# Weight halves all on VectorE, a count in PSUM, and a later routing set-up

## The chip, the cores and the metric

The kernel runs on one core of a Trainium2 chip. A core has TensorE (PE), which multiplies matrices into PSUM, VectorE (DVE), ScalarE (ACT), GpSimd (POOL) and SyncE (SP); they run side by side, each through its own list of instructions in order, and wait for one another by semaphores. Here SP issues the loads and most stores, and POOL the indirect gathers and scatters. The metric is the device time of one execution in microseconds (us).

## The reference

Three layers follow one another, all in float32 (B = 2, S = 768, width D = 384):

```python
# 1 gated linear attention, 8 heads of 48
for t in range(S):
    state = alpha[:, :, t, :, None] * state + einsum('bhd,bhe->bhde', k[:, :, t], v[:, :, t])
    y[:, :, t] = einsum('bhd,bhde->bhe', q[:, :, t], state)
# 2 mixer: a token layer (d_tok 256), a channel layer (d_ch 1536)
u = x + (relu(x^T @ w_tok1) @ w_tok2)^T
z = u + relu(u @ w_ch1) @ w_ch2
# 3 experts: 8 of 384 -> 1024 -> 384, one for each token
logits = z @ w_gate;  local = sigmoid(z @ w_local)
e = argmax(logits) if local < 0.5 or s == 0 else e of the token before
out = softmax(logits)[e] * (relu(z @ w1[e]) @ w2[e])
```

## The kernel before

**Products in parts.** Where float32 precision is wanted, `parts` (L337) makes one product of three: high half by high half, high by low, low by high. Every weight is split on its way: ACT casts the raw tile to the high half (L333), and an engine that the call of `split` names subtracts it from the raw tile, which gives the low half (L334, a TENSOR_TENSOR with both inputs in SBUF). Activations are split likewise: ACT writes `hh`, DVE `hl` (L509 and L510 in the mixer, L820 and L821 in the experts); there one of the inputs lies in PSUM.

**Attention** runs over 16 half-steps (2 batches, 4 pairs of heads, 2 halves of the sequence). Per half SP loads a block with decays, keys and queries (L180), and `v` (L184) once for both halves. DVE makes two scans (L191, L197), POOL scales keys and queries (L217, L218), PE makes scores, states and outputs, with products of ones between them in the first half-steps (L164). The tables for the routing are made in `route_setup`, the gate's weights loaded in `route_load` (L569). A few products of the mixer's first layer (`mix_hiddens`) are issued in the last half-steps.

**Mixer.** The token layer for both batches, then the channel layer over groups of 384 tokens (`h` and `a` products of L337). While it runs, the tokens of earlier groups are routed, and the first expert's weights arrive (`expert_weights`): of each expert three tiles of `w1` and four of `w2`, each tile in two halves. DVE takes the low halves of `w1` and of the even halves of `w2`, POOL those of the odd ones.

**Closing** is the end of the mixer: the last 384 tokens leave the channel layer (sums `a` by PE, `u` of L489 by DVE, `x2d` stored by SP), and are routed one group of 128 after the other, in a chain of small operations through PE, DVE and ACT (L612 to L717). Beside it `close` starts expert 0 on the tokens it already has; `fill_half` (L889) counts how many places are left over there, on one element (L893 to L899). Around it three tiles of expert 1's weights are split, with `w1_eng` set to POOL for the low halves.

**Experts** 1 to 7 have two tiles of 128 tokens each. PE makes a hidden product `h` per 128 of the 1024 hidden units, and adds its second product into `o` one or two steps later; DVE's `y` (L807) is scattered to the output by POOL (L729). Gathers (L725) fetch the tokens. `more_passes` and L1253 look whether a further pass is needed, again on one element.

**Order.** The program is written per stage with priorities and `issue_after` bounds; a scheduler turns it into one list per engine. Tile names are those of the buffers, so that weights of different experts appear as c0h, c1h, x0h, x1h, th (high) and c0l, c1l, x0l, x1l, tl (low).

Of the kernel before, what the change touches and what calls it, by code (L numbers as in the profile page):

```python
# [10 lines left out]
ALU = mybir.AluOpType  # L11
AX = mybir.AxisListType

P = 128
# [5 lines left out]
NG = 2  # L20
# [13 lines left out]
KD = DM // P  # L34
# [57 lines left out]
class Build:  # L92
# [79 lines left out]
    def attention_load(self, h):  # L172

        nc, n = self.nc, h["n"]
        x = self.ring[n % len(self.ring)][:DQ]
        src = self.i["akq"][h["b"], h["p"], h["g"]]
        cuts = [0, NA + 1, NA + 1 + SG, NA + 1 + 2 * SG]

        for lo, hi in zip(cuts, cuts[1:]) if n == 0 else [(0, cuts[3])]:
            nc.sync.dma_start(x[:, lo:hi], src[:, lo:hi])  # L180
        h["alpha"], h["k"], h["q"] = [x[:, lo:hi] for lo, hi in zip(cuts, cuts[1:])]
        if h["g"] == 0:
            h["v"] = self.vs[n // NG % len(self.vs)]
            nc.sync.dma_start(h["v"], self.i["v"][h["b"], h["p"]].rearrange("t c (j d) -> t c j d", j=2))  # L184

    def att_decay(self, h):

# [96 lines left out]
    def attention(self, x, between):  # L284
        hs = []
        for b in range(B):
            for p in range(NP):
                for g in range(NG):
                    hs.append({"b": b, "p": p, "g": g, "x": x, "n": len(hs)})
        n = len(hs)  # L290
        state = None

        def load(h):
            self.attention_load(h)
            if h["g"]:
                h["v"] = hs[h["n"] - 1]["v"]

        def decay(h):

            after = hs[0].get("scaled" if h["n"] == 1 else "scored") if h["n"] in (1, 2) else None  # L300
            with self.tc.issue_after(after.ins) if after is not None else nullcontext():
                self.att_decay(h)

        def add(h):
            nonlocal state

            with self.tc.issue_after(hs[min(h["n"] + 2, n - 1)]["back"].ins):
                state = self.att_state(h, state if h["g"] else None)

        stages = {"L": load, "D": decay, "I": self.att_back, "Q": self.att_scale,  # L310
                  "K": self.att_knat, "C": self.att_scores, "S": add, "O": self.att_out}
        done = set()

        def go(x, k):
            if 0 <= k < n and (x, k) not in done:
                done.add((x, k))
                with self.tc.high_priority(offset=PRI[x]) if x in PRI else nullcontext():
                    stages[x](hs[k])

        for x in "LDIQ":  # L320
            go(x, 0)
        for i in range(-5, n):
            for x in ORDER.split():
                go(x[0], i + int(x[1:]))
            if i >= 0:
                between(i, hs)
# [409 lines left out]
    def expert_weights(self, experts, to):  # L736


        nc = self.nc

        def load(j):
            e, i = experts[j // STEPS_W], j % STEPS_W
            pool, tag, bufs = self.stages[j % len(self.stages)]
            if i < KD:
                x = self.t(pool, [P, FF], tag, bufs=bufs)
                src = self.i["moe2_w1"][bass.ds(e, 1)]
                nc.sync.dma_start(x, src[:, i * P:(i + 1) * P].rearrange("o p f -> p (o f)"))
            else:
                f = 2 * (i - KD)
                x = self.t(pool, [P, 2, DM], tag, bufs=bufs)  # L750
                src = self.i["moe2_w2"][bass.ds(e, 1)]
                nc.sync.dma_start(x, src[:, f * P:(f + 2) * P].rearrange("o (k p) d -> p (o k) d", p=P))
            return x

        got = []
        for n in range(len(experts)):
            n1, n2 = self.ROOM[n % len(self.ROOM)]
            size = KF // len(n2)
            for i in range(STEPS_W):
                while len(got) < len(self.stages) and n * STEPS_W + i + len(got) < len(experts) * STEPS_W:  # L760
                    got.append(load(n * STEPS_W + i + len(got)))
                x = got.pop(0)
                if i == 0:
                    w1 = [self.big_tile(n1 + y, [P, KD, FF], F32R) for y in "hl"]
                    w2, rest = [], []
                    to[n] += [w1, w2, rest]
                if i < KD:
                    for m in range(0, FF, PART):
                        ms = slice(m, m + PART)
                        self.split(w1[0][:, i, ms], w1[1][:, i, ms], x[:, ms], self.w1_eng)  # L770
                else:
                    for f in range(2):
                        if len(w2) == 2 * (i - KD) + f:
                            room = size if len(n2) == 1 else NT
                            h, l = [self.big_tile(n2[len(w2) // size] + y, [P, room, DM], F32R) for y in "hl"]
                            w2 += [(h[:, k], l[:, k]) for k in range(size)]
                            if room > size:
                                rest += [y[:, size:].rearrange("p n d -> p (n d)") for y in (h, l)]
                        self.split(*w2[2 * (i - KD) + f], x[:, f], nc.gpsimd if f else nc.vector)
                yield  # L780

    def expert_input(self, xs, to):
# [106 lines left out]
    def fill_half(self):  # L889

        nc, t, rp = self.nc, self.t, self.rtp
        ps = self.room(1)
        nc.tensor.matmul(ps[0:1], self.onesb[:, 0:1], self.count[:, 0:1], start=True, stop=True)  # L893
        more = t(rp, [P, 1], "fill")
        nc.vector.tensor_scalar(more[0:1], ps[0:1], -1.0, float(P), ALU.mult, ALU.add)
        nc.vector.tensor_scalar(more[0:1], more[0:1], 0.0, None, ALU.max)
        x = t(rp, [P, E], "sum", BF16, bufs=CG)
        nc.vector.tensor_copy(x, self.count)
        nc.vector.tensor_tensor(x[0:1, 0:1], x[0:1, 0:1], more[0:1], ALU.add)  # L899
        self.count = x  # L900
# [157 lines left out]
    def mixer_and_experts(self, x, r0, weights):  # L1058


        nc = self.nc
        self.stages = [(self.stp, "part", 2), (self.stp, "raw64", 2)] * 2
        self.ahead = AHEAD
        self.w1_eng = nc.vector
        with self.phase():
            self.mixp = self.pool("mix", 2)
            self.psh = self.pool("ps_h", 2, space=PSUM)
# [51 lines left out]
            def aside(n, m):  # L1119
                if n == 0:  # L1120
                    more()
                if n + 1 < B * NG and 3 <= m < 3 + CG:
                    if m == 3:
                        turns[n] = self.turn(us[n + 1], uts[n + 1])
                    next(turns[n])
                if n and m:
                    if m == 1:
                        routes[n] = self.route((n - 1) * CG, [us[n - 1][:, c] for c in range(CG)], self.room)
                    next(routes[n], None)
                if n and m % 3 == 0:  # L1130
                    if next(later, None) is not None:
                        next(stream)
                if n == B * NG - 1 and m == CLOSE:
                    early.append(self.close(ws[0]))
                    next(early[0])
                if n == B * NG - 1 and m == MC - 1:

                    self.w1_eng = nc.gpsimd
                    for _ in range(AHEAD_W):
                        next(stream)  # L1140
                    self.w1_eng = nc.vector

            chains, weighs, early = [], [], []

# [147 lines left out]
def mixed(ctx, tc, ins, out):  # L1292
# [16 lines left out]
    with z.phase():  # L1309
        z.attention_setup()  # L1310
        z.bits = lambda: z.t(z.psp["bits"], [P, PART], "bits")
        z.warm_up(WARM)
        steps = B * NP * NG

        def between(i, hs):
            if i == 1:
                z.route_setup()
                z.route_load()
            if i == 0:
                next(weights)  # L1320
            if i % 2 and i // 2 < EARLY:
                with tc.high_priority(offset=-BEHIND), tc.issue_after(hs[min(i + 3, steps - 1)]["back"].ins):
                    next(weights)
            if i == NP * NG - 1:
                x.append(inputs(1))
            if i == steps - 5:
                z.load_to = 12
            if i == steps - 3:

                r = z.hidden_room()  # L1330
                ahead.extend((r, z.mix_hiddens(x[0], lambda: z.t(z.psp["r"], [P, 512], "r")[:, :DM], r)))
            if i >= steps - 3:
                for _ in range(KT * NT // 3):
                    next(ahead[1])

        z.attention(x, between)
        for _ in ahead[1]:
            pass
        z.bad_decay()
# [49 lines left out]
```

## Time and profile before

| what | value |
|---|---|
| time, median of 3 runs | 459.81 us (457.43 to 463.89) |
| profiled execution, its own time | 459.7 us |
| its span, first to last instruction | 458.0 us |
| PE busy | 428.0 us (93%) |
| DVE, ACT, POOL busy | 284.1, 178.9, 149.0 us |
| DMA | 56.11 MB, 123 GB/s on average |

The span leaves out what lies before the first and after the last instruction, here 1.7 us. Busy times overlap: they don't add up to the span. A row of a timeline gives start and length, and in brackets how long the engine had been idle and what released it; an instruction that takes several times as long as others of its shape, with no idle time before it, was held up while it ran.

### The profile page before, as it was taken

How to read it: one execution, taken by the hardware profiler on the slowest of the kernel's cores; microseconds unless marked ns; L12 is line 12 of the kernel's file. 1: busy time of each engine (PE TensorE's matmuls, PEld its weight loads, DVE VectorE, ACT ScalarE, POOL GpSimd, SP SyncE). 2: the span in 40 equal slices, each digit the busy share in tenths (PEclk: the TensorE clock that was granted, in tenths of full speed). 3: DMA queues.
4: the chain of work that ended last, by engine and by line, in shares of the span. 5: the costliest groups of instructions: out<-in, count | busy, mean ns of one | idle time of the engine just before them, and what ended most of it. 6: DMA issues, size and time to landing. Idle time of an engine off the chain costs nothing. (4 is left out here: it accounts for less than half of the span.)

```text
span 458.0 us, 7912 instructions
## 1 busy us (share of the span) xinstructions
PE 428.0 (93%) x2938; PEld 387.6 (85%) x2938; DVE 284.1 (62%) x672; ACT 178.9 (39%) x439; POOL 149.0 (33%) x169
## 2 busy tenths in 40 slices
PE   6999999999999999999999985999898998998991
PEld 3577788779999999999999975678888998998990
DVE  5999993499994335134431475666977968928320
ACT  3646664323355231122112140256655555625210
POOL 3767772443442000000000033077527325405010
PEclk9899999999999999999999997999999999999996
DMA  8999976141348300010001004059777847410010
GB/s 213 259 250 247 240 281 230 48 136 47 93 135 252 115 1 0 1 52 1 0 8 47 1 10 133 34 181 281 207 242 247 254 135 247 134 37 28 3 45 24
DMA packets 27921, 56.11 MB, mean 123 GB/s; under 512 B 3556, under 2 KB 18284, under 8 KB 27872
## 3 DMA queue, kind: packets, MB, share of 16 engines
q1 hardware_dynamic: 25824, 50.78, 38.0%
q0 software_dynamic: 2048, 4.72, 3.1%
q8 instruction: 25, 0.41, 0.4%
q14 instruction: 24, 0.20, 0.1%
HBM read 51.55 MB, written 5.51 MB: 125 GB/s over the span
## 5 line engine op out<-in xcount | busy, mean ns | idle before, releaser
L510 DVE SCALAR_TENSOR_TENSOR hl<-h,hh 128x384 fp32r<-128x384 f32 x45 | 25.0, 556 | 57.7 <-ACT hh L509 57.5
L509 ACT ACTIVATE hh<-h 128x384 fp32r<-128x384 f32 x45 | 22.1, 490 | 69.4 <-PE h L337 61.8
L725 POOL DMA_INDIRECT early_y<-x2d,early x1 | 1.2, 1228 | 120.2 <-DVE share L600 120.2
L337 PE MATMUL a<-c2h,hl 128*128 128x384 f32 x87 | 29.5, 339 | 6.3 <-DVE hl L510 6.3
L337 PE MATMUL h<-uh,c0h 128*128 128x384 f32 x96 | 34.8, 362 | 0.0
L729 POOL DMA_INDIRECT out_dram<-y,ids x14 | 14.5, 1037 | 61.8 <-DVE y L807 19.9
L337 PE MATMUL h<-uh,c0l 128*128 128x384 f32 x96 | 32.6, 339 | 0.0
L337 PE MATMUL h<-ul,c0h 128*128 128x384 f32 x96 | 32.3, 337 | 0.0
L337 PE MATMUL a<-c2h,hh 128*128 128x384 f32 x87 | 29.4, 338 | 0.0
L337 PE MATMUL a<-c2l,hh 128*128 128x384 f32 x87 | 29.2, 336 | 0.0
L821 DVE SCALAR_TENSOR_TENSOR hl<-h,hh 128x256 fp32r<-128x256 f32 x48 | 20.0, 416 | 13.8 <-ACT hh L820 13.8
L820 ACT ACTIVATE hh<-h 128x256 fp32r<-128x256 f32 x48 | 18.4, 383 | 24.8 <-PE h L337 24.7
L276 PE MATMUL y<-c0h,at 128*128 128x48 f32 x192 | 27.3, 265 | 0.0
L276 PEld LDWEIGHTS y<-c0h,at 128*128 128x128 f32 x192 | 25.3, 191 | 0.1
L164 PE MATMUL r<-onesb 128*128 128x512 bf16 x76 | 23.9, 425 | 1.3 <-DVE onesb L128 1.3
L337 PE MATMUL h<-xh,c0h 128*128 128x256 f32 x72 | 21.2, 295 | 3.8 <-DVE hl L821 3.3
L243 POOL TENSOR_SCALAR_AFFINE_SELECT at<-at 128x384 f32<-128x384 f32 x32 | 16.0, 524 | 20.5 <-ACT at L242 20.5
L337 PEld LDWEIGHTS a<-c2h,hl 128*128 128x128 f32 x87 | 16.4, 189 | 6.6 <-DVE hl L510 6.6
L337 PE MATMUL h<-xl,c0h 128*128 128x256 f32 x72 | 20.2, 280 | 0.0
L337 PE MATMUL h<-xh,c0l 128*128 128x256 f32 x72 | 20.1, 280 | 0.0
L334 DVE TENSOR_TENSOR c1l<-raw,c1h 128x384 fp32r<-128x384 f32 x11 | 19.6, 1808 | 0.4 <-issue 0.2
L220 ACT ACTIVATE qs<-qn,inv 112x128 f32<-112x128 f32 x48 | 16.1, 392 | 7.1 <-POOL qn L217 4.2
(395 smaller groups left out, 1380.1 us busy)
## 6 DMA issues: line engine op xcount, KB each, us to landing
raw<-in_moe_w_dram SPq DMA_DIRECT2D x22, 384.0 KB
raw<-in_moe_w_dram SPq DMA_DIRECT2D x15, 512.0 KB
part<-in_moe_w_dram SPq DMA_DIRECT2D x9, 512.0 KB
part<-in_moe_w_dram SPq DMA_DIRECT2D x10, 384.0 KB
c2l<-in_akq_dram SPq DMA_DIRECT2D x6, 505.8 KB
x1l<-in_moe_w_ch_dram SPq DMA_DIRECT2D x5, 512.0 KB
c2h<-in_akq_dram SPq DMA_DIRECT2D x5, 505.8 KB
c0h<-in_v_dram SPq DMA_DIRECT2D x8, 288.0 KB
```

Source lines behind the costliest of these rows:

```text
L164: self.nc.tensor.matmul(ps, self.onesb, self.onesb.unsqueeze(1).to_broadcast([P, 512 // P, P]), start=True, stop=True)
L220: nc.scalar.activation(qs[:DQ, c], qn[:DQ, c], AF.Copy, scale=h["inv"][:, c])
L243: nc.gpsimd.affine_select(at, at, [[0, CG], [1, P]], ALU.is_ge, 0.0, base=0, channel_multiplier=-1)
L276: last = nc.tensor.matmul(y[:, c, j * D:(j + 1) * D], h["at"][j][:, c], h["v"][:, g * CG + c, j], start=state is None, stop=state is None ...
L334: eng.tensor_tensor(lo, x, hi.bitcast(F32), ALU.subtract)
L337: self.last = self.nc.tensor.matmul(*args, **kw)
L509: nc.scalar.activation(hh, ps, AF.Relu)
L510: nc.vector.scalar_tensor_tensor(hl, ps, 0.0, hh.bitcast(F32), ALU.max, ALU.subtract)
L725: return self.nc.gpsimd.indirect_dma_start(xs, None, self.x2d[:rows], bass.IndirectOffsetOnAxis(ids, 0), bounds_check=rows - 1, oob_is_err ...
L729: self.nc.gpsimd.indirect_dma_start(self.out, bass.IndirectOffsetOnAxis(ids[:, a], 0), y, None, bounds_check=TB * P - 1, oob_is_err=False)
L820: nc.scalar.activation(hh, ps, AF.Relu)
L821: nc.vector.scalar_tensor_tensor(hl, ps, 0.0, hh.bitcast(F32), ALU.max, ALU.subtract)
```

## The change

Five edits, in the order of the diff:

- `attention_load` issues the load of `v` with the second half of a pair of heads instead of the first.
- `expert_weights` gives every low half to DVE; `w1_eng` is gone, also from closing.
- `fill_half` keeps its count (`more`) in a second column of the PSUM tile in which the sum arrives, not in an SBUF tile.
- `route_setup` and `route_load` are issued at half-step 12 of 16, not 1.
- Of the early products of `mix_hiddens` a third is issued at half-step 14 and the rest after attention; before, a third at each of half-steps 13, 14 and 15.

```diff
@@ -179,9 +179,11 @@
         for lo, hi in zip(cuts, cuts[1:]) if n == 0 else [(0, cuts[3])]:
             nc.sync.dma_start(x[:, lo:hi], src[:, lo:hi])
         h["alpha"], h["k"], h["q"] = [x[:, lo:hi] for lo, hi in zip(cuts, cuts[1:])]
-        if h["g"] == 0:
-            h["v"] = self.vs[n // NG % len(self.vs)]
-            nc.sync.dma_start(h["v"], self.i["v"][h["b"], h["p"]].rearrange("t c (j d) -> t c j d", j=2))
+
+        if h["g"]:
+            v = self.vs[n // NG % len(self.vs)]
+            nc.sync.dma_start(v, self.i["v"][h["b"], h["p"]].rearrange("t c (j d) -> t c j d", j=2))
+            return v
 
     def att_decay(self, h):
 
@@ -291,9 +293,9 @@
         state = None
 
         def load(h):
-            self.attention_load(h)
+            v = self.attention_load(h)
             if h["g"]:
-                h["v"] = hs[h["n"] - 1]["v"]
+                h["v"] = hs[h["n"] - 1]["v"] = v
 
         def decay(h):
 
@@ -767,7 +769,7 @@
                 if i < KD:
                     for m in range(0, FF, PART):
                         ms = slice(m, m + PART)
-                        self.split(w1[0][:, i, ms], w1[1][:, i, ms], x[:, ms], self.w1_eng)
+                        self.split(w1[0][:, i, ms], w1[1][:, i, ms], x[:, ms], nc.vector)
                 else:
                     for f in range(2):
                         if len(w2) == 2 * (i - KD) + f:
@@ -776,7 +778,7 @@
                             w2 += [(h[:, k], l[:, k]) for k in range(size)]
                             if room > size:
                                 rest += [y[:, size:].rearrange("p n d -> p (n d)") for y in (h, l)]
-                        self.split(*w2[2 * (i - KD) + f], x[:, f], nc.gpsimd if f else nc.vector)
+                        self.split(*w2[2 * (i - KD) + f], x[:, f], nc.vector)
                 yield
 
     def expert_input(self, xs, to):
@@ -889,10 +891,11 @@
     def fill_half(self):
 
         nc, t, rp = self.nc, self.t, self.rtp
-        ps = self.room(1)
-        nc.tensor.matmul(ps[0:1], self.onesb[:, 0:1], self.count[:, 0:1], start=True, stop=True)
-        more = t(rp, [P, 1], "fill")
-        nc.vector.tensor_scalar(more[0:1], ps[0:1], -1.0, float(P), ALU.mult, ALU.add)
+
+        ps = self.room(2)
+        more = ps[:, 1:2]
+        nc.tensor.matmul(ps[0:1, 0:1], self.onesb[:, 0:1], self.count[:, 0:1], start=True, stop=True)
+        nc.vector.tensor_scalar(more[0:1], ps[0:1, 0:1], -1.0, float(P), ALU.mult, ALU.add)
         nc.vector.tensor_scalar(more[0:1], more[0:1], 0.0, None, ALU.max)
         x = t(rp, [P, E], "sum", BF16, bufs=CG)
         nc.vector.tensor_copy(x, self.count)
@@ -1061,7 +1064,6 @@
         nc = self.nc
         self.stages = [(self.stp, "part", 2), (self.stp, "raw64", 2)] * 2
         self.ahead = AHEAD
-        self.w1_eng = nc.vector
         with self.phase():
             self.mixp = self.pool("mix", 2)
             self.psh = self.pool("ps_h", 2, space=PSUM)
@@ -1134,11 +1136,8 @@
                     early.append(self.close(ws[0]))
                     next(early[0])
                 if n == B * NG - 1 and m == MC - 1:
-
-                    self.w1_eng = nc.gpsimd
                     for _ in range(AHEAD_W):
                         next(stream)
-                    self.w1_eng = nc.vector
 
             chains, weighs, early = [], [], []
 
@@ -1313,7 +1312,7 @@
         steps = B * NP * NG
 
         def between(i, hs):
-            if i == 1:
+            if i == steps - 4:
                 z.route_setup()
                 z.route_load()
             if i == 0:
@@ -1329,7 +1328,8 @@
 
                 r = z.hidden_room()
                 ahead.extend((r, z.mix_hiddens(x[0], lambda: z.t(z.psp["r"], [P, 512], "r")[:, :DM], r)))
-            if i >= steps - 3:
+            if i == steps - 2:
+
                 for _ in range(KT * NT // 3):
                     next(ahead[1])
```

In closing, on DVE. `fill` and `r` are `more` of L895 to L902 before and after, `hl` is the split that PE's next product takes, `c0l` a low half of expert 1's `w1`. Before:

```order
L1009 SCALAR_TENSOR_TENSOR early_3036<-tab_368 128x1
L600 TENSOR_TENSOR share_369<-share_369,r_3014 128x16
L1013 COPY early_s_3042<-share_369 128x1
L895 TENSOR_SCALAR fill_3027<-r_3025 1x1
L896 TENSOR_SCALAR fill_3027<-fill_3027 1x1
L899 TENSOR_TENSOR sum_3030<-sum_3030,fill_3027 1x1
L510 SCALAR_TENSOR_TENSOR hl_3055<-h_3044,hh_3054 128x384
L489 TENSOR_TENSOR u_1444<-a_574_2753,u_1444 128x384
L841 TENSOR_TENSOR u_3033<-t_3111,u_3033 128x384
```

With the change (lines are two or three higher there):

```order
L1016 COPY early_s_3041<-share_1062 128x1
L336 TENSOR_TENSOR c0l_3060<-raw_488_2275,c0h_3059 128x512
L898 TENSOR_SCALAR r_3025<-r_3025 1x1
L336 TENSOR_TENSOR c0l_3060<-raw_488_2275,c0h_3059 128x512
L899 TENSOR_SCALAR r_3025<-r_3025 1x1
L512 SCALAR_TENSOR_TENSOR hl_3054<-h_3043,hh_3053 128x384
L902 TENSOR_TENSOR sum_3029<-sum_3029,r_3025 1x1
L336 TENSOR_TENSOR c0l_3060<-part_2392,c0h_3059 128x512 x2
L336 TENSOR_TENSOR c0l_3060<-raw_535_2511,c0h_3059 128x512 x2
L491 TENSOR_TENSOR u_1444<-a_574_2753,u_1444 128x384
L491 TENSOR_TENSOR u_1444<-a_575_2754,u_1444 128x384
```

The six low halves of POOL stand on DVE now, two ahead of `hl`, four behind the sum on one element, which went behind `hl`.

On DVE in the experts, where expert 3's `w2` (c1l) is split beside the last steps of the expert before. Before:

```order
L807 TENSOR_SCALAR y_3852<-o_748_3552,share_369 128x384
L807 TENSOR_SCALAR y_3860<-o_749_3556,share_369 128x384
L334 TENSOR_TENSOR c1l_3933<-part_3707,c1h_3932 128x384
L334 TENSOR_TENSOR c1l_3933<-raw_778_3748,c1h_3932 128x384
L821 SCALAR_TENSOR_TENSOR hl_3893<-h_3882,hh_3892 128x256
L334 TENSOR_TENSOR c1l_3933<-raw_3781,c1h_3932 128x384
L334 TENSOR_TENSOR c1l_3933<-raw_3827,c1h_3932 128x384
L821 SCALAR_TENSOR_TENSOR hl_3921<-h_3910,hh_3920 128x256
```

With the change:

```order
L809 TENSOR_SCALAR y_3851<-o_747_3551,share_1062 128x384
L809 TENSOR_SCALAR y_3859<-o_748_3555,share_1062 128x384
L336 TENSOR_TENSOR c1l_3932<-part_3706,c1h_3931 128x384 x2
L823 SCALAR_TENSOR_TENSOR hl_3892<-h_3881,hh_3891 128x256
L336 TENSOR_TENSOR c1l_3932<-raw_777_3747,c1h_3931 128x384 x2
L336 TENSOR_TENSOR c1l_3932<-raw_3780,c1h_3931 128x384 x2
L823 SCALAR_TENSOR_TENSOR hl_3920<-h_3909,hh_3919 128x256
L336 TENSOR_TENSOR c1l_3932<-raw_3826,c1h_3931 128x384
L794 TENSOR_TENSOR xl_3938<-x_3939,xh_3937 128x256
L336 TENSOR_TENSOR c1l_3932<-raw_3826,c1h_3931 128x384
L336 TENSOR_TENSOR c0l_4081<-raw_3929,c0h_4080 128x512
L823 SCALAR_TENSOR_TENSOR hl_3955<-h_3944,hh_3954 128x256
```

Two of the low halves that POOL had stand between one `hl` and the next; up to four low halves follow one another there.

At the start, on SP (c2h, c2l, c1l: blocks of decays, keys and queries; c0h: `v`). Before:

```order
L180 DMA c2h_116<-in_akq_dram 112x388
L180 DMA c2h_116<-in_akq_dram 112x384 x2
L184 DMA c0h_119<-in_v_dram 128x576
L180 DMA c2h_116<-in_akq_dram 112x1156
L180 DMA c2l_117<-in_akq_dram 112x1156
L184 DMA c0h_119<-in_v_dram 128x576
L180 DMA c2l_117<-in_akq_dram 112x1156
L180 DMA c1l_118<-in_akq_dram 112x1156
```

With the change:

```order
L180 DMA c2h_116<-in_akq_dram 112x388
L180 DMA c2h_116<-in_akq_dram 112x384 x2
L180 DMA c2h_116<-in_akq_dram 112x1156
L185 DMA c0h_119<-in_v_dram 128x576
L180 DMA c2l_117<-in_akq_dram 112x1156 x2
L185 DMA c0h_119<-in_v_dram 128x576
L180 DMA c1l_118<-in_akq_dram 112x1156 x2
```

`v` stands behind the second half's block. The two loads of the gate's weights (L569), which followed some rows later among these loads, come behind the last load of the token layer's weights.

## Rows read from the trace of the kernel before

**Rows 1.** Per core: span and mean granted TensorE clock.

```profile
core 0: 458.0 us, clock 0.981
```

**Rows 2.** Waits of PE: who waits for whom, total us, times, longest.

```profile
PE h L337 <- DVE hl L821: 6.5, 6, 2.1
PE a L337 <- DVE hl L510: 6.3, 1, 6.3
...
PE h L337 <- DVE c2l L334: 0.5, 1, 0.5
```

**Rows 3.** Windows: length, busy us (x instructions) per engine, PEclk, DMA share.

```profile
275.00:280.00 5.00, 0.45 (x1) 0.45 (x2) 4.50 (x2) 0.00 (x0) 4.01 (x4) 0.70 0.49 157
280.00:285.00 5.00, 5.00 (x24) 4.81 (x23) 0.82 (x2) 0.96 (x2) 0.00 (x0) 0.61 0.45 147
285.00:290.00 5.00, 5.00 (x32) 4.17 (x32) 2.71 (x17) 0.93 (x4) 0.00 (x0) 1.00 0.11 39
```

**Rows 4.** Timeline of DVE, closing: start us, us, engine, line, operation [idle before <-releaser].

```profile
271.06 7.97 DVE L899 TENSOR_TENSOR sum<-sum,fill 1x1 bf16<-1x1 bf16 x1
278.96 0.54 DVE L510 SCALAR_TENSOR_TENSOR hl<-h,hh 128x384 fp32r<-128x384 f32 x1
```

**Rows 5.** Timeline of POOL, closing.

```profile
271.62 2.53 POOL L334 TENSOR_TENSOR c0l<-raw,c0h 128x512 fp32r<-128x512 f32 x2
```

**Rows 6.** Timeline of PE, closing: the stall, and the mixer's last product.

```profile
279.55 0.69 PE L337 MATMUL a<-c2h,hl 128*128 128x384 f32 x1 [6.27 <-DVE hl L510]
...
290.26 0.34 PE L337 MATMUL a<-c2h,hl 128*128 128x384 f32 x1
```

**Rows 7.** Timeline of ACT, closing.

```profile
271.00 0.48 ACT L509 ACTIVATE hh<-h 128x384 fp32r<-128x384 f32 x1
```

**Rows 8.** DVE groups by shape: xcount | busy us, mean ns | idle before.

```profile
L334 DVE TENSOR_TENSOR c1l<-raw,c1h 128x384 fp32r<-128x384 f32 x11 | 19.6, 1808 | 0.4 <-issue 0.2
...
L334 DVE TENSOR_TENSOR c0l<-raw,c0h 128x512 fp32r<-128x512 f32 x8 | 5.2, 684 | 2.2 <-ACT c0h L333 2.2
```

**Rows 9.** Timeline of DVE, experts.

```profile
306.10 0.55 DVE L334 TENSOR_TENSOR c1l<-part,c1h 128x384 fp32r<-128x384 f32 x1
...
310.75 0.42 DVE L792 TENSOR_TENSOR xl<-x,xh 128x256 fp32r<-128x256 f32 x1 [0.61 <-ACT xh L791]
...
327.85 3.17 DVE L1253 TENSOR_TENSOR more<-passes,bad 1x1 f32<-1x1 f32 x1
...
340.17 1.29 DVE L334 TENSOR_TENSOR c0l<-raw,c0h 128x512 fp32r<-128x512 f32 x2 [2.18 <-ACT c0h L333]
...
344.03 4.05 DVE L334 TENSOR_TENSOR c1l<-raw,c1h 128x384 fp32r<-128x384 f32 x2
```

**Rows 10.** Timeline of POOL, experts.

```profile
306.06 1.00 POOL L725 DMA_INDIRECT xs<-x2d,ids  x1 [0.30 <-issue]
...
310.42 1.02 POOL L334 TENSOR_TENSOR c1l<-part,c1h 128x384 fp32r<-128x384 f32 x1
```

**Rows 11.** Timeline of PE, experts: the first product after each longer stall.

```profile
332.88 0.38 PE L337 MATMUL h<-xh,c0h 128*128 128x256 f32 x1 [2.06 <-DVE hl L821]
...
341.85 0.39 PE L337 MATMUL h<-xh,c2h 128*128 128x256 f32 x1 [0.30 <-DVE hl L821]
...
348.47 0.39 PE L337 MATMUL h<-xh,c2h 128*128 128x256 f32 x1 [1.68 <-DVE hl L821]
...
385.00 0.38 PE L337 MATMUL h<-xh,c0h 128*128 128x256 f32 x1 [1.27 <-DVE hl L821]
...
418.94 0.39 PE L337 MATMUL h<-xh,th 128*128 128x256 f32 x1 [1.01 <-DVE hl L821]
```

**Rows 12.** Timeline of DVE, the first scan.

```profile
9.07 0.96 DVE L191 TENSOR_TENSOR_SCAN f<-c2h,one 112x387 f32<-112x387 f32 x1 [2.21 <-DMA c2h<-in_akq_dram]
```

**Rows 13.** The page's slices, 11.45 us each: GB/s.

```profile
GB/s 213 259 250 247 240 281 230 48 136 47 93 135 252 115 1 0 1 52 1 0 8 47 1 10 133 34 181 281 207 242 247 254 135 247 134 37 28 3 45 24
```

**Rows 14.** The page's DMA issues: KB each.

```profile
c0h<-in_v_dram SPq DMA_DIRECT2D x8, 288.0 KB
```

## The prediction

> **What bounds the kernel now.** First the span and clock per core: 458.0 us at a mean clock of 0.981 [rows 1]. The profiled execution took 459.7 us, 0.1 below the median of the three runs, so I add up against 459.7. TensorE is busy for 428.0 of the 458.0 us, so time can only come out of the 30 us in which it stands still, or out of stretches at a low clock. The view of TensorE's waits tells where most of those are: 6.5 us in six stalls behind `hl` of the experts, and 6.3 us in one stall behind `hl` of the mixer [rows 2]. Nothing else in that view comes near them.
>
> Both groups have one origin, which the timelines of VectorE and GpSimd show side by side. In closing an addition on a single element takes 7.97 us on VectorE, from 271.06 to 279.0 [rows 4], exactly as long as GpSimd works through the six low halves that begin at 271.62 [rows 5]: three such rows of 2.5 us each, two instructions a row, which end at 279.0. `hl`, which TensorE wants, stands behind that addition, and itself takes 0.54 us [rows 4]. In the experts the subtraction of a low half has a mean of 1808 ns in one group of VectorE [rows 8], and 0.55 us at 306.10, where GpSimd makes no arithmetic [rows 9]. Two of them took 4.05 us together, and a 1x1 addition 3.17 us [rows 9]. The common trait of the held instructions is two inputs in SBUF. `xl`, whose one input lies in PSUM, took its usual 0.42 us at 310.75 [rows 9], while GpSimd ran a low half from 310.42 to 311.4 [rows 10]. So it isn't VectorE's work that is too long, but that the two engines lock each other out.
>
> **The change part by part.**
>
> *Closing.* Two edits remove the same stall. With the count in PSUM the 1x1 addition has one input in SBUF left, as `xl` has; and with the low halves on VectorE nothing runs on GpSimd that could hold it. What VectorE gets instead is six low halves of 684 ns [rows 8], 4.1 us. Two of them stand ahead of `hl`. The high half of the activation is ready at 271.5 [rows 7]. The 1x1 operations before the addition were done at 271.06 [rows 4]; two low halves (1.4) and `hl` (0.54) more give 273.0. TensorE runs out of work at 279.55 less 6.27, which is 273.28 [rows 6]: `hl` comes 0.3 us early, and the whole 6.27 us goes. After the stall the clock was low, 0.70 and 0.61 in two stretches of 5 us, in the second with 24 products where the next stretch, at full clock, has 32 [rows 3]. Eight missing products of 5/32 us make 1.25 us, which go as well, since without the idle time nothing gives the clock a cause to fall. That makes 7.5. Against it stand the other four low halves, 2.7 us ahead of the first `u` on VectorE: they end near 275.8, when TensorE still has some 5 us of sums for the tokens that follow. I take 0.5 off for small routing steps that now wait behind the sums. **7.0 us**, between 5.5 (the last `u` and the chain behind it late by 2 us) and 7.5. The mixer's last product would start at 283.3 instead of 290.26 [rows 6].
>
> *Experts.* Of 28 low halves of 128x384, four in each of seven experts, 0.55 us of VectorE each come to its account, 2.2 us per expert. Four more, which were split in the mixer while TensorE had no waits, count as nothing: VectorE's work there is covered by TensorE's products; without that cover they cost 2.2 us. The long stalls of TensorE are 2.06, 1.68, 1.27 and 1.01 us [rows 11]; with one of 0.30, and a last of 0.2 that the total leaves, they make the 6.5. The stall of 2.06 ends behind the 1x1 addition of 3.17 us, the one of 1.68 behind the two low halves of 4.05 us [rows 9]; the others are of that second kind. Only the one of 0.30 is another: there at 340.17 VectorE had waited 2.18 us for ACT's cast of a tile that had just landed [rows 9]. So 6.2 us hang on the lock. What can come in its place is short: at most four low halves between one `hl` and the next, 2.2 us, about as long as TensorE takes from one hidden product to the next. I keep 1.2 for it: **5.0 us**, between 2 (a new 0.6 us in each expert) and 6.2.
>
> *Loads of `v`.* VectorE's first scan waits 2.21 us for its block at 9.07 [rows 12]; the second half's block, the first that moves, now goes ahead of 288 KB of `v` [rows 14]. At 213 GB/s in the first slice [rows 13] these are 1.4 us: the second scan's data land that much earlier, `v` that much later, and `v` is wanted only when keys are scaled and scores made. But TensorE also has its products of ones there, which are its own work. **0.9 us**, between a gain of 1.4 and a loss of 1.0, if `v` is late for the first state.
>
> *Set-up and early products.* The order shows that VectorE's set-up operations hardly move, some rows at the start; the two small loads leave SP's list of attention loads. The early products only change places with others in a stretch where the waits name nothing for TensorE. **0**, between +1.3 (a wait like the longest of the middle ones, 1.27 [rows 11]) and -0.4.
>
> Sum: 459.7 - 7.0 - 5.0 - 0.9 = **446.8 us**. With the gains at their lower bounds it is 459.7 - 5.5 - 2.0 + 1.0 + 1.3 = 454.5, at their upper ones 459.7 - 7.5 - 6.2 - 1.4 - 0.4 = 444.2.
>
> **A rule that speaks against it.** GpSimd keeps its gathers and scatters, and VectorE becomes busier beside them. In the trace a gather at 306.06 takes 1.00 us [rows 10] while a low half on VectorE at 306.10 takes 0.55 us [rows 9], the usual time of both: they don't hold each other up, and the sum has no term for it. The Trainium skill, "SBUF — State Buffer", section "🔬 SBUF: two separate sides", warns of the opposite: a DMA issued by GpSimd can't get its descriptors written while VectorE is in an operation that takes both port pairs, such as a float32 copy within SBUF. By it the copies and casts, not the subtractions, would hold the gathers, and no copy is added here.
>
> **The rivals.**
> - *Only closing gains.* The waits of the experts stay, as waits in VectorE's order: the low halves wait for ACT's casts, these for loads. For it: the 0.5 us behind c2l [rows 2] and the 0.30 us stall are of that kind. Against it: the four long stalls aren't. 459.7 - 7.0 - 0.9 = 451.8.
> - *The chain of closing takes the place.* The last tokens' routing is a chain of small steps, and if it, not the sums, sets the start of the experts, half of closing's gain is lost: 459.7 - 3.5 - 5.0 - 0.9 = 450.3. Against it: it starts from `u`, which comes as much earlier.
> - *The gathers are held.* Were each of 14 gathers late by one low half of 0.55 us, with half of it uncovered, this gives back 3.9: 450.7. The page named above has it only for other operations; the gather at 306.06 speaks against it.
> - *The change doesn't do what it says.* VectorE is held by something else, as the gather of expert 0's tokens, which still runs beside the 1x1 addition: 459 to 460. Against it: the hold ends with the sixth low half.
> - *Slower: VectorE's order becomes the bound.* Each of the 28 low halves that came over waits on VectorE for a cast that waits for its load, as at 340.17, and `hl` behind it is late by the 0.5 us of [rows 2]: 14 us more, 446.8 + 14.0 = 460.8. It decides from 12.9/28 = 0.46 us per low half. Against it: such waits are two in the whole phase now, and VectorE's lists are shorter in time without the lock.
>
> **How the numbers follow.** Two per cent, about what a measurement of this kernel can tell from no change, lie at 450.6. The forecast has 0.64 (nearly all of it below), the closing chain 0.10 (0.07 below), only closing 0.12 (0.04 below), the gathers 0.04 (0.02 below), no effect 0.06, VectorE's bound 0.04 (0.03 above by over 2%). That makes 0.76 faster, 0.21 the same, 0.03 slower. The range reaches from below the upper bound of the gains, with the scatter of the three runs (457.43 to 463.89) on one side, 442.5, to the other side of *only closing*, 453.5; beyond it lie the last two cases and the ends of the others, under 2 in 10.
>
> **What would show it.** The 1x1 addition at 0.15 us instead of 7.97, no stall of TensorE behind the mixer's `hl`, full clock from 275 to 290, and the mixer's last product near 282 (with the start's gain). No group of low halves on VectorE above 0.7 us; TensorE's waits behind the experts' `hl` below 1.5 us together. The second scan over 1 us earlier. Wrong it would be if new waits behind `hl` or c0l to c2l have several us together, if the gathers grow beyond 1.2 us, or if the experts begin less than 5 us earlier.

## The result and the profile after

The changed kernel takes 444.13 us (median of 4 runs, 442.69 to 463.58), the kernel before in the same runs 461.85 (457.43 to 466.99): a ratio of 0.9637, interval 0.9523 to 0.975. In a second set of runs it was 0.9643 (0.9583 to 0.9704). Some executions of either kernel have a lower mean clock, as that of 463.58 us (0.950), and in the three traces of such executions (e1_count, e4_start, e9_nofront) TensorE stands at the lower of its two levels, 0.50 (1.2 GHz), for 17 us and more between 34 and 120 us of the span: the ratios leave those executions out, and of the three traces only what lies outside that stretch is read. The profiled execution took 442.69 us. Its span, against [rows 1]:

```profile
core 0: 440.7 us, clock 0.990
```

First the row that answers to [rows 2]. Waits of TensorE, in the same columns; the first is now the longest of its rows, and lies in the first half-steps of attention, at 15.5 us:

```profile
PE ds L255 <- DVE st L264: 1.4, 1, 1.4
...
PE h L339 <- DVE hl L823: 0.4, 1, 0.4
```

The stall behind the mixer's `hl` is gone, the six behind the experts' `hl` are one of 0.4 us. In closing, where [rows 4] have the addition of 7.97 us, VectorE now does this:

```profile
269.54 0.69 DVE L336 TENSOR_TENSOR c0l<-raw,c0h 128x512 fp32r<-128x512 f32 x1 [0.20 <-PE h L339]
270.14 0.15 DVE L898 TENSOR_SCALAR r<-r 1x1 f32<-1x1 f32 x1
270.21 0.67 DVE L336 TENSOR_TENSOR c0l<-raw,c0h 128x512 fp32r<-128x512 f32 x1
270.81 0.15 DVE L899 TENSOR_SCALAR r<-r 1x1 f32<-1x1 f32 x1
270.88 0.53 DVE L512 SCALAR_TENSOR_TENSOR hl<-h,hh 128x384 fp32r<-128x384 f32 x1
271.34 0.14 DVE L902 TENSOR_TENSOR sum<-sum,r 1x1 bf16<-1x1 bf16 x1
271.41 1.27 DVE L336 TENSOR_TENSOR c0l<-part,c0h 128x512 fp32r<-128x512 f32 x2
272.61 1.27 DVE L336 TENSOR_TENSOR c0l<-raw,c0h 128x512 fp32r<-128x512 f32 x2
```

The addition (L902) takes 0.14 us. `hl` begins at 270.88, with two low halves ahead of it and four behind, all at their usual length. The scheduler has also put `hl` ahead of the addition, so that here it would pass even if the addition were held; that the addition isn't held is read from its own 0.14 us. TensorE passes without a stop, at full clock, as the windows show that answer to [rows 3] (length, then busy us of PE, PEld, DVE, ACT, POOL, then PEclk, DMA share, GB/s), and makes the mixer's last product 9.12 us earlier than in [rows 6]:

```profile
271.00:276.00 5.00, 5.00 (x34) 4.76 (x32) 3.66 (x8) 2.29 (x5) 0.00 (x0) 1.00 0.84 197
276.00:281.00 5.00, 5.00 (x32) 3.80 (x32) 2.69 (x18) 1.31 (x6) 0.00 (x0) 1.00 0.50 169
```

```profile
281.14 0.34 PE L339 MATMUL a<-c2h,hl 128*128 128x384 f32 x1
```

In the experts, the groups of [rows 8] by shape, and on the timeline of VectorE the 1x1 addition that took 3.17 us in [rows 9], and four low halves in a row:

```profile
L336 DVE TENSOR_TENSOR c1l<-raw,c1h 128x384 fp32r<-128x384 f32 x22 | 11.3, 550 | 0.0
...
L336 DVE TENSOR_TENSOR c0l<-raw,c0h 128x512 fp32r<-128x512 f32 x12 | 7.9, 679 | 2.9 <-ACT c0h L335 2.7 <-PE h L339 0.2
```

```profile
321.49 0.14 DVE L1252 TENSOR_TENSOR more<-passes,bad 1x1 f32<-1x1 f32 x1
...
331.97 1.95 DVE L336 TENSOR_TENSOR c1l<-raw,c1h 128x384 fp32r<-128x384 f32 x4
```

The mean of c1l fell from 1808 to 550 ns, although there are twice as many of them.

Where the time came from is best read by laying equal instructions of the two timelines over each other. `hl` that opens closing (269.36 before) is 1.05 us earlier, the experts' first `hl` (314.06 before) 9.81, their last (439.95 before) 17.65. So the front gave 1.05, closing with the experts' beginning 8.76 and the rest of the experts 7.84; behind their last `hl` 0.4 is lost again, which leaves 17.2 of the span.

### The profile page after: what moved, and what is told of

The parts are those of the page before. It is cut to its first block, busy times and chain, and to the rows that moved or that the text cites. A ratio compares the mean times of both kernels' runs of the same rounds, so it can differ in the third digit from the quotient of the medians.

```text
span 440.7 us, 7862 instructions
## 1 busy us (share of the span) xinstructions
PE 423.6 (96%) x2938; PEld 385.2 (87%) x2938; DVE 272.4 (62%) x710; ACT 178.5 (41%) x439; POOL 108.2 (25%) x131
## 5 line engine op out<-in xcount | busy, mean ns | idle before, releaser
L731 POOL DMA_INDIRECT out_dram<-y,ids x14 | 14.2, 1016 | 88.0 <-DVE y L809 67.1
L339 PEld LDWEIGHTS h<-uh,c0h 128*128 128x128 f32 x96 | 18.0, 188 | 0.8
L339 PEld LDWEIGHTS h<-ul,c0h 128*128 128x128 f32 x96 | 18.1, 188 | 0.0
```

The lines of the kernel that those rows point to most:

```text
L339: self.last = self.nc.tensor.matmul(*args, **kw)
L731: self.nc.gpsimd.indirect_dma_start(self.out, bass.IndirectOffsetOnAxis(ids[:, a], 0), y, None, bounds_check=TB * P - 1, oob_is_err=False)
```

## The experiments

The theory is that VectorE's operations with two inputs in SBUF are shut out while GpSimd does arithmetic. Its rivals: the addition waits for something else that ends when the sixth low half does, or the experts gain by weights that are ready sooner.

**The count alone.** The hunk of the change on `fill_half`, and nothing else:

```diff
-        ps = self.room(1)
-        nc.tensor.matmul(ps[0:1], self.onesb[:, 0:1], self.count[:, 0:1], start=True, stop=True)
-        more = t(rp, [P, 1], "fill")
-        nc.vector.tensor_scalar(more[0:1], ps[0:1], -1.0, float(P), ALU.mult, ALU.add)
+        ps = self.room(2)
+        more = ps[:, 1:2]
+        nc.tensor.matmul(ps[0:1, 0:1], self.onesb[:, 0:1], self.count[:, 0:1], start=True, stop=True)
+        nc.vector.tensor_scalar(more[0:1], ps[0:1, 0:1], -1.0, float(P), ALU.mult, ALU.add)
```

> Only the count goes into PSUM; GpSimd keeps all its low halves. Theory (VectorE's operations with two SBUF inputs are shut out while GpSimd does arithmetic): the 1x1 addition takes 0.15 us although GpSimd's six low halves of closing run beside it, TensorE's stall of 6.3 us behind the mixer's hl goes, the experts keep their six stalls of 6.5 us; span 458.0 - 8.0 = 450, ratio near 0.983. Rival (the addition waits for something else that ends with the sixth low half, or GpSimd's halves only come late): the addition still takes about 8 us, span near 458.

Ratio 0.9861 (0.9759 to 0.9963), which alone leaves open whether the gain reaches 2%; the trace decides. VectorE's and GpSimd's timelines in closing, and TensorE's wait in the experts:

```profile
282.29 0.14 DVE L900 TENSOR_TENSOR sum<-sum,r 1x1 bf16<-1x1 bf16 x1
282.73 0.56 DVE L510 SCALAR_TENSOR_TENSOR hl<-h,hh 128x384 fp32r<-128x384 f32 x1 [0.29 <-ACT hh L509]
```

```profile
281.58 1.23 POOL L725 DMA_INDIRECT early_y<-x2d,early  x1 [121.12 <-DVE share L600]
282.85 2.56 POOL L334 TENSOR_TENSOR c0l<-raw,c0h 128x512 fp32r<-128x512 f32 x2
```

```profile
PE h L337 <- DVE hl L821: 5.4, 5, 2.0
```

The addition starts 0.56 us ahead of GpSimd's first low half (282.29 and 282.85), as it does in the kernel before (271.06 and 271.62), behind the same instructions and beside the same gather; only the place of one operand differs from [rows 4], and it takes 0.14 us instead of 7.97. It is over before that half begins in the rows. What runs beside it is `hl`, with one input in PSUM, at its usual 0.56. The experts' stalls are five of 5.4 us instead of six of 6.5, which is within what traces with these experts show (4.1 to 7.3, below). From closing's `hl` to the experts' first one this kernel is 9.3 us shorter than the one before, from there to the last one it is the same (0.05). The rival on closing is out.

**A smaller dose.** The kernel before, but two of closing's six low halves given to VectorE, behind `hl`:

```diff
-                    for _ in range(AHEAD_W):
+                    for k in range(AHEAD_W):
+                        self.w1_eng = nc.vector if k == 1 else nc.gpsimd
                         next(stream)
```

> The kernel before with four of closing's six low halves on GpSimd and two on VectorE behind hl; the count in SBUF. Theory (the addition is shut out for as long as GpSimd works): 7.97 - 2 x 1.25 = 5.5 us for the addition, TensorE's stall 6.3 - 2.5 = 3.8 us. Rival (the addition waits for a fixed thing, as the gather beside it): still near 8 us.

The addition on VectorE, the four low halves on GpSimd, and TensorE's product behind `hl`:

```profile
278.67 5.54 DVE L899 TENSOR_TENSOR sum<-sum,fill 1x1 bf16<-1x1 bf16 x1
```

```profile
279.23 4.95 POOL L334 TENSOR_TENSOR c0l<-raw,c0h 128x512 fp32r<-128x512 f32 x4
```

```profile
284.73 0.45 PE L337 MATMUL a<-c2h,hl 128*128 128x384 f32 x1 [3.79 <-DVE hl L510]
```

5.54 us and 3.79 us, against 5.5 and 3.8 expected: the hold ends with GpSimd's last low half, at 284.2. The one execution took 465.31 us, with closing 7.6 us later than in the kernel before; it is read for closing alone.

**The odd halves of w2 alone** on VectorE, so that closing is as before:

```diff
-                        self.split(*w2[2 * (i - KD) + f], x[:, f], nc.gpsimd if f else nc.vector)
+                        self.split(*w2[2 * (i - KD) + f], x[:, f], nc.vector)
```

> Only the odd halves of w2 move to VectorE; in closing GpSimd keeps its six low halves of w1, and the count stays in SBUF. Theory: the 1x1 addition still takes about 8 us and TensorE stalls 6.3 us, the experts' stalls behind hl fall from 6.5 to under 1 us; span 458.0 - 8.6 = 449.5, ratio near 0.981. Rival (the gain of the experts came from closing's earlier end, or from weights that are ready sooner there): the experts' stalls stay above 3 us and the span is above 453.

Ratio 0.9807 (0.9708 to 0.9906). VectorE's addition in closing, and TensorE's waits:

```profile
271.36 7.97 DVE L899 TENSOR_TENSOR sum<-sum,fill 1x1 bf16<-1x1 bf16 x1
```

```profile
PE a L337 <- DVE hl L510: 6.2, 1, 6.2
...
PE h L337 <- DVE hl L821: 0.9, 1, 0.9
```

The addition is the same to the hundredth of a microsecond, and the experts gain without it: 6.45 us from their first `hl` to their last, 1.2 more ahead of that. So their gain doesn't come from closing's earlier end. Nor does it come from gathers that GpSimd issues sooner without the low halves: in the kernel before, TensorE waited for a gather of the experts only once, for 0.3 us.

**All low halves on VectorE**, the count in SBUF (both lines of `expert_weights`; with them goes `w1_eng`, as in the change):

```diff
-                        self.split(w1[0][:, i, ms], w1[1][:, i, ms], x[:, ms], self.w1_eng)
+                        self.split(w1[0][:, i, ms], w1[1][:, i, ms], x[:, ms], nc.vector)
...
-                        self.split(*w2[2 * (i - KD) + f], x[:, f], nc.gpsimd if f else nc.vector)
+                        self.split(*w2[2 * (i - KD) + f], x[:, f], nc.vector)
```

> All low halves on VectorE, the count stays in SBUF, start as before. Theory: both stalls go without the PSUM edit, since GpSimd has no arithmetic left beside them; closing 8.0 and the experts 8.6 us shorter, span about 441.5, ratio near 0.965. Rival (the PSUM edit is needed in closing): the 1x1 addition stays long and the span is near 449.

Ratio 0.9629 (0.9535 to 0.9724): as much as the whole change. On VectorE, behind `hl`:

```profile
270.40 0.54 DVE L510 SCALAR_TENSOR_TENSOR hl<-h,hh 128x384 fp32r<-128x384 f32 x1
270.86 0.14 DVE L899 TENSOR_TENSOR sum<-sum,fill 1x1 bf16<-1x1 bf16 x1
```

The addition has both inputs in SBUF, as before, and takes 0.14 us, since GpSimd has no arithmetic beside it. Either edit alone ends closing's stall.

**The count and w2's odd halves**, GpSimd keeping closing's six, and **the change without the front's edits**; on the same chip as the second run of the changed kernel:

> Count in PSUM and the odd halves of w2 on VectorE; GpSimd keeps the six low halves of closing, and the front is as before. Theory (the lock needs two SBUF inputs on VectorE beside arithmetic on GpSimd): closing's halves on GpSimd hurt nobody, the addition takes 0.15 us, closing and experts gain as in the changed kernel, time equal to it within 1%. Rival (VectorE has to take closing's halves too, since expert 1's weights would come late from GpSimd): a stall of 1 us or more behind c0l at expert 1, time 1 to 3 us above.

> The changed kernel without the three edits at the front (v, set-up, early products). If they are worth the 0.9 us of the sum, this is 0.9 us above the changed kernel; if what the traces of the mixer's start show is only scatter of the front from run to run (-1.6 to +0.3 us with the same front), the two are equal within their scatter of 1 us.

> The changed kernel once more, on the chip of the next two. Ratio 0.96 to 0.965, stalls behind the mixer's hl none and behind the experts' hl 0.4 us.

The ratios are 0.9654 (0.9585 to 0.9722) for the first, 0.9679 (0.9596 to 0.9762) for the second and 0.9643 for the changed kernel: equal within their intervals. In the first, GpSimd keeps its halves, the addition ahead of them takes 0.14 us, and no wait of TensorE for c0l is in its trace in closing or at expert 1:

```profile
274.04 0.14 DVE L900 TENSOR_TENSOR sum<-sum,r 1x1 bf16<-1x1 bf16 x1
```

```profile
274.60 2.56 POOL L334 TENSOR_TENSOR c0l<-raw,c0h 128x512 fp32r<-128x512 f32 x2
```

The hunk on `fill_half` and one line of `expert_weights` have the gain; no version here beats the changed kernel by more than the scatter (medians 444.76 and 443.60 us on this chip). The three times of the second that count have a median of 444.42, 0.8 us above the changed kernel, and go from 442.07 to 446.35, so that a term of 0.9 us can't be told from nothing in them. The second run of the changed kernel showed no wait behind the experts' `hl` in the rows, against 0.4 expected.

**The front.** All three edits together, and each alone:

> Only the three edits at the front: v with the second half, the set-up at half-step 12, the early products at half-step 14. Forecast by the sum: 0.9 us shorter from the load of v, the other two nothing; as the changed kernel's trace has it, its mixer was 1.1 us earlier. Span 456.9 to 457.2, both long stalls as before, the same within the measurement. Rival: the 1.1 us came from the lock's end (four low halves that GpSimd had in the mixer) and the span is 458.

> Only the load of v goes behind the second half's block. Theory: the second scan starts about 1 us earlier than in traces without this edit (8.6 to 10.0 us in seven of them, 8.0 to 8.2 in three with all front edits), that is at 8.2; by the mixer the gain is lost in the scatter of the front. Both long stalls stay. Rival (the set-up's later place gave the earlier scan): the scan stays at 9 us or later.

> Only the routing set-up and the gate's load are issued at half-step 12. Theory: the second scan stays at 8.6 to 10 us, VectorE's set-up casts stay among the first scans, since the order hardly moves them, and TensorE's first wait for a state stays. Rival: the casts move behind the attention's first half-steps and the third scores come 1 us or more earlier.

> Only the early products of the mixer move. Theory: no wait of TensorE is added or removed between 70 and 100 us beyond 0.4, both long stalls as before. Rival: a wait of 1 us or more of TensorE between the end of attention and the mixer's first layer.

Of the first a single time counts, 458.15 us, within the scatter of the kernel before (456.09 to 462.09 in those runs); one run can't confirm the forecast. Its trace has closing's stall of 6.3 us, and 4.1 us in four stalls of the experts. The other three ran once each (463.59, 466.06 and 461.76 us), all with closing's stall of 6.2 us; no time of theirs bears on a term of 0.9 us. What follows calls the scan of L191 that belongs to the second half-step the second scan; [rows 12] and the prediction call it the first, which begins at 3.23 us. It is shown for the changed kernel, with v alone and with the set-up alone, and in two kernels that have the front as before (e2_lows and e8_few):

```profile
8.07 0.96 DVE L193 TENSOR_TENSOR_SCAN f<-c2h,one 112x387 f32<-112x387 f32 x1 [1.56 <-DMA c2h<-in_akq_dram]
```

```profile
8.71 0.96 DVE L193 TENSOR_TENSOR_SCAN f<-c2h,one 112x387 f32<-112x387 f32 x1 [1.33 <-DMA c2h<-in_akq_dram]
```

```profile
9.42 0.96 DVE L191 TENSOR_TENSOR_SCAN f<-c2h,one 112x387 f32<-112x387 f32 x1 [2.40 <-DMA c2h<-in_akq_dram]
```

```profile
8.60 0.96 DVE L191 TENSOR_TENSOR_SCAN f<-c2h,one 112x387 f32<-112x387 f32 x1 [2.21 <-DMA c2h<-in_akq_dram]
```

```profile
9.98 0.96 DVE L191 TENSOR_TENSOR_SCAN f<-c2h,one 112x387 f32<-112x387 f32 x1 [2.34 <-DMA c2h<-in_akq_dram]
```

With all three edits it begins at 7.98 to 8.19 us in three traces, in seven with none of them at 8.60 to 9.98. With v alone it came at 8.71, not at 8.2 as expected, which is still inside the others' scatter; with the set-up alone at 9.42, and the casts stay between the scans, as the order has it. With the early products alone TensorE waits 0.5 us for a state at 71.3 us, a little over the 0.4 expected, and at most 0.35 us where the mixer begins; the rival's 1 us isn't there. What of it arrives is another matter. The place of closing's first `hl`, against the kernel before: -1.05 and +0.73 in the two traces of the changed kernel, -1.54 (e2_lows), +0.30 (e3_w2) and +2.98 (e8_few) with the front as before. Whatever the front's edits are worth is smaller than this.

## Why the prediction was right

The forecast was 446.8 us, from a profile of 459.7; it came out at 444.13, inside the range. For closing and the experts path and mechanism were right, the sizes too small: the two terms that carry the sum passed their own upper bounds of 7.5 and 6.2 us, the result lies at the 444.2 that the sum gives with every gain at its upper bound, and the range reaches beyond it only by the scatter that was added. The mechanism is shown: the same addition with the operand moved (e1_count), with GpSimd's work moved (e2_lows), and with a part of it (d1_four). Term by term:

- **Closing, 7.0 forecast, 8.8 measured** in the changed kernel up to the experts' first `hl`, 8.1 up to the mixer's last product (9.12 less the front's 1.05). The idle 6.27 us and the full clock came back (34 and 32 products per 5 us, against 24). The product behind `hl`, at 279.55 in [rows 6], now starts here:

```profile
272.06 0.34 PE L339 MATMUL a<-c2h,hl 128*128 128x384 f32 x1
```

That is 7.49 earlier, 6.4 without the front; so about 1.6 came back behind the stall, where 1.25 was worked out for the low clock. The 0.5 us taken off for small routing steps was not lost. The gap of 0.5 behind c2l [rows 2], beside the experts' first `hl`, also went, but it is in no other trace either, not even with closing and experts as before (e5_v, e6_setup, e7_hidden), and so is no gain of the change. From closing's first `hl` to the experts' first one the six traces with the stall of 6.2 us or more take 43.5 to 45.2 us, the six without 35.4 to 37.7.
- **Experts, 5.0 forecast, 7.8 measured** (8.5 in the second trace of the changed kernel, 7.0 and 6.45 in e2_lows and e3_w2). This is the term that was most mis-sized. The 6.5 us of stalls that it starts from are one trace's: behind the experts' `hl` the seven traces in which GpSimd has the odd halves show 4.1 to 7.3 us, the six in which it hasn't 0 to 0.9. From the experts' first `hl` to their last the former take 125.0 to 127.0 us, the latter 117.4 to 119.4, so that the 7.8 holds to about 1 us. The 1.2 us kept for a queue of low halves ahead of `hl` was not lost: four in a row took 1.95 us, and the only wait is 0.4. And a stall costs more than the idle time beside it says. Here are, of the kernel before, TensorE's last transposes ahead of the stall of 1.27 us [rows 11], whose product started at 385.00, and then the same transposes and product in the changed kernel:

```profile
383.35 0.38 PE L790 MATMUL x<-ident,xs 128*128 128x128 f32 x2
```

```profile
366.91 0.38 PE L792 MATMUL x<-ident,xs 128*128 128x128 f32 x2
367.05 0.37 PE L339 MATMUL h<-xh,c0h 128*128 128x256 f32 x1
```

Before, the product starts 1.65 us behind the transposes (383.35 to 385.00), after 0.14 us: the stall of 1.27 us costs 1.51, since without it products overlap. Were it 0.24 more for each of the six, that would be 1.4 us (an estimate from this one), which with the 6.1 us of idle time that went comes near the 7.8.
- **Loads of v, 0.9 forecast: not shown.** No run shows this term. The second scan does come earlier in the three traces with all edits, but the front varies by more than 4 us between traces with one and the same code, and the 1.05 us of the changed kernel is no evidence for the term.
- **Set-up and early products, 0 forecast:** nothing else was found.
- **The four low halves of the mixer, nothing forecast:** from 150 to 250 us the distance between the two kernels' `hl` stays at 1.1 us.

Of the rivals, *only closing gains* and *VectorE's order becomes the bound* needed waits behind the low halves that didn't come: c0l's group waited 2.7 us for ACT in all, and TensorE 0.4. *The chain of closing* started from `u` as much earlier as the sums: closing's last `u` by 9.12 us, from 290.64 to 281.52. *The gathers are held* is out by their mean times on GpSimd, before and after:

```profile
L725 POOL DMA_INDIRECT xs<-x2d,ids x14 | 15.6, 1116 | 6.2 <-PE x L790 3.0 <-issue 2.6 <-POOL xs L1249 0.3
L729 POOL DMA_INDIRECT out_dram<-y,ids x14 | 14.5, 1037 | 61.8 <-DVE y L807 19.9 <-ACT c1h L333 19.5 <-ACT x1h L333 11.1
```

```profile
L727 POOL DMA_INDIRECT xs<-x2d,ids x14 | 14.6, 1042 | 11.0 <-PE x L792 8.1 <-issue 2.1 <-DMA out_dram<-y,ids 0.3
L731 POOL DMA_INDIRECT out_dram<-y,ids x14 | 14.2, 1016 | 88.0 <-DVE y L809 67.1 <-DVE hl L823 5.4 <-DVE c1l L336 4.8
```

They fell a little, 1116 to 1042 ns and 1037 to 1016 ns, beside more subtractions on VectorE. The warning that the prediction quoted from the Trainium skill is not tested by these runs, as none of them adds a copy. What they do bear out is the Trainium skill, "SBUF — State Buffer", section "Who interferes with whom": a VectorE instruction with two SBUF inputs contends with a GpSimd instruction that reads SBUF, and one with a single SBUF input doesn't, outside the two-port modes that the page names. Here that is 7.97 us against 0.14 ahead of the same work of GpSimd, and `hl` at 0.56 beside it.

## What to carry to other kernels

Read an instruction that takes many times its usual length, with no idle time before it, as held by another engine, and look on GpSimd's timeline for work that ends with it; then ask how many of its operands lie in SBUF. To move one operand into PSUM was enough in closing, though GpSimd kept its work there. And cost a stall of TensorE from start to start of the products around it, as the overlap that it breaks isn't in the idle time.

## What the runs showed of the hardware

- VectorE's addition wasn't served between two subtractions of GpSimd: over six of about 1.25 us, and over four, it waited until the last had ended, 7.97 and 5.54 us.
- The hold began before GpSimd's first recorded half: the addition starts 0.56 us ahead of it in both (271.06 and 271.62; 278.67 and 279.23), so that it doesn't last exactly as long as GpSimd's six halves, as the prediction has it. In the experts the addition at 327.85 [rows 9] was held likewise, by subtractions recorded from 328.06. GpSimd's gather, which runs at that time in closing, doesn't hold by itself: in the changed kernel two subtractions on VectorE with both inputs in SBUF, at 269.54 and 270.21, take their usual 0.69 and 0.67 us, the first wholly beside it.

```profile
269.31 1.23 POOL L727 DMA_INDIRECT early_y<-x2d,early  x1 [133.78 <-DVE share L602]
```

What holds in those 0.56 us the rows don't show.
- TensorE's clock stood at 0.70 and 0.61 over 5 us each around the stall of 6.27 us [rows 3]; from 300 to 450 us, around the experts' stalls of up to 2.06 us, no window of 5 us was below full clock.
